# First six units' logits quad by quad, and list one-hots as 16-bit outer products with GpSimd's help

## The chip, the cores and the metric

The kernel runs on one core of a Trainium2 chip. The metric is the device time of one execution in microseconds; the median of several runs is given. TensorE (PE) multiplies matrices, VectorE (DVE) and ScalarE (ACT) work on tiles in SBUF and PSUM, GpSimd (POOL) does small copies and starts the indirect transfers, and SyncE (SP) starts most plain transfers. Each engine works its own queue in order; semaphores tie the queues together.

## The reference

```python
# x: (8, 2880, 192), 23040 tokens of 192; weight: 8 heads x 7 taps
w = softmax(weight)                                  # per head
out[b, s, h, :] = sum_k w[h, k] * x_pad[b, s + k, h, :]     # causal convolution per head
# mixture of experts: 4 groups x 4 experts, F = 1024
g_idx = argmax(x @ w_group);  g_w = softmax(x @ w_group)[g_idx]
e_idx = argmax(x @ w_expert[g_idx]);  e_w = softmax(...)[e_idx]
ye = relu(x @ w1[g, e]) @ w2[g, e]
out[token] = g_w * e_w * ye
```

Each token is convolved, sent to one of 16 experts by two argmaxes, and the expert's output is scaled by both probabilities.

## The kernel before

Tokens are taken in blocks of 120 (`BT`), and blocks in units: six units of 4, 8, 12, 8, 8 and 8 blocks, then twelve of 12 (u0 to u17). `unit(u)` is a generator whose steps are interleaved with those of other units and, later, with the experts' work; the order of instructions on each engine is fixed when the program is built.

A unit goes through these stages. Its eight heads are convolved on PE as products with a banded matrix (L452), and ACT copies them to the tile `xc` (L461). There are three `xc` buffers; u0 and u1 share one, so u4 takes the buffer of u0 and u1, u5 that of u2, u6 that of u3, and so on. Four blocks at a time (a quad), the tokens are transposed to `ta` and `tb` (`turn_a` L475, `turn_b` L483). `logits` (L495, L497) multiplies all quads of the unit by the router's weights with the weights stationary, and ACT copies the result to `lts` (L500), `logits_back` transposes it back quad by quad (L507), and ACT copies it to `lg` (L508): 20 logits for each token. DVE finds the maxima and one-hots (L539 to L551), ACT takes the Exp (L545), DVE the sums and the reciprocal (L562 to L568), which goes into `xc` as each token's factor. ACT's queue then starts the store of `xc` to `xcd` in DRAM (L570).

The lists of tokens for each expert are made as follows. A scan counts within the unit (L557), two small matmuls (L579, L580) count over the partitions, and DVE works out each token's place in the list of its expert (L583 to L595). The place is split into a row (128 of them) and a column (32). DVE makes one-hots of the row (`ohl`, L608) and of the column (`ohr`, L615), multiplies the latter by the token's number (`ohv`, L619), in halves of six blocks, and PE sums their products over the blocks (L633). The result (`lv`, `lsi`, L640, L642) is scattered by POOL to the table `idtab` (L645), at rows given by `rowi`. `rowi` (L624 to L626) needs only the counts up to the unit before, so it is placed early, and each scatter waits for the landing of the one before. The table is cleared ahead of the first scatter (`clear_table`, L269, L272, from a tile filled with a large number).

When five units are routed (`NEED`), the first portion of the lists is loaded (`idp`, L1157, SP) and POOL gathers the tokens of the first slots from `xcd` (`xg`, L717). A slot is 256 tokens of one expert: two transposes into `xa` and `xb` (L750, L752), hidden layer (L817 or L786, `ph`), relu and splitting into `hh` and `hl` (ACT, DVE, four buffers), output layer (L835, L839, or L801, L805), the factor (`ys`, L898) and POOL's scatter to `out` (L888). All matmuls of the experts are made of parts, so weights are split on arrival (`ah`, `al`, `bh`, `bl`, `cw`). From then on slots and the steps of the remaining units alternate, and after the last unit come the tail's slots.

Of the kernel before, what the change touches and what calls it, by code (L numbers as in the profile page):

```python
# [36 lines left out]
def conv_moe_kernel(  # L37
# [227 lines left out]
    fill = pa.tile([P, HB2, P], F16, name="ohl", bufs=2).rearrange("p b q -> p (b q)").bitcast(I32)  # L265
# [110 lines left out]
    quads = [-1] * QRING  # L376
    read = {-1}
# [20 lines left out]
    def gaps(u):  # L398

        return tuple(UG[3 * u:3 * u + 3]) if 3 * u < len(UG) else (GA, GL, REST)  # L400

    def unit(u, pre=None):
# [86 lines left out]
        def logits():  # L489
# [8 lines left out]
            read.add(u)  # L498
# [74 lines left out]
        while any(need <= u and pi not in idps for need, pi in needs.items()):  # L573
# [20 lines left out]
            out=posb[0:Q, 0], in0=pn, scalar1=-(LH - 1) / 2, scalar2=RND, op0=ALU.add, op1=ALU.add)  # L594
        nc.vector.scalar_tensor_tensor(  # L595
            out=posb[0:Q, 1], in0=posb[0:Q, 0], scalar=RND, in1=pn, op0=ALU.subtract, op1=ALU.subtract)

        halves = []
        for b0 in range(0, nb, HB2):
            n = min(HB2, nb - b0)  # L600
            if u >= LP and b0:
                for _ in range(HGAP):
                    yield
            ohl = pa.tile([P, HB2, P], F16, name="ohl", bufs=2)
            ohr = rt.tile([P, HB2, LH], F16, name="ohr", bufs=1)
            ohv5 = pa.tile([P, HB2, LH], F16, name="ohv", bufs=2)
            bs = slice(b0, b0 + n)
# [4 lines left out]
            if u >= LP:  # L612
                for _ in range(LG):
                    yield
            hold(u >= LP, nc.vector.tensor_tensor(  # L615
                out=ohr[0:Q, 0:n], in0=ior[0:Q].unsqueeze(1).broadcast_to([Q, n, LH]), in1=bc(posb[0:Q, 1, bs], LH),
                op=ALU.is_equal,
            ))
# [12 lines left out]
        for b0, n, ohl, ohv5 in halves:  # L631
            for k in range(n):
                nc.tensor.matmul(  # L633
                    out=pl[:, 0:nrep * LH].rearrange("p (r n) -> p r n", r=nrep), lhsT=ohl[0:Q, k],
                    rhs=ohv5[0:Q, k].unsqueeze(1).broadcast_to([Q, nrep, LH]),
                    start=b0 + k == 0, stop=b0 + k == nb - 1,
                )
# [246 lines left out]
    def finish(oo, ids, xs, hold=False, rare=False):  # L884
        ys = ff.tile([P, 2, D], F32, name="ysr" if rare else "ys", bufs=1 if rare else YB)
# [603 lines left out]
```

## Time and profile before

| what | value |
|---|---|
| median of 3 runs | 1145.09 us (1145.08 to 1145.1) |
| profiled execution | 1152.26 us, of which the profile's span is 1150.4 us |
| PE busy | 1072.8 us (93%) |
| DVE, ACT, POOL busy | 752.4, 644.1, 523.5 us |
| mean granted PE clock | 0.977 of full speed |
| transferred | 166.08 MB, mean 144 GB/s |

PE is busy for most of the span, and less so near its start. Busy shares are means over stretches with different limits, so the rows below go by stretch.

### The profile page before, as it was taken

The numbers are of one execution on the slowest core, as the hardware profiler recorded it, in microseconds if no ns is written. First come the engines' busy times: TensorE is split into PE (matmuls) and PEld (weight loads), VectorE is DVE, ScalarE is ACT, GpSimd is POOL, SyncE is SP. The second block draws the span as 40 slices with busy tenths as digits, with TensorE's granted clock in tenths as the row PEclk, the third lists the DMA queues.
The fourth block names the chain that finished last, engine by engine and source line by source line (L and its number), as shares of the span: only waits on it lengthen the run. The fifth ranks groups of instructions, "written<-read, shape, count | busy, mean of one in ns | idle before, by whom it ended". The sixth has DMA issues, their size and how long they took to land.

```text
span 1150.4 us, 20931 instructions
## 1 busy us (share of the span) xinstructions
PE 1072.8 (93%) x7124; PEld 971.1 (84%) x7124; DVE 752.4 (65%) x1671; ACT 644.1 (56%) x1362; POOL 523.5 (46%) x611
## 2 busy tenths in 40 slices
PE   6565999998999998999999999999999999999996
PEld 4444788987989998889899999999999988989986
DVE  3465878987778756576565555655556665687874
ACT  5445657765657554454455445554545555677873
POOL 3004143333334454554545454545445554487773
PEclk9878989999999999999999999999999999999998
DMA  8767688999566432332253223322333435499970
GB/s 185 186 158 228 160 222 215 252 234 216 156 155 164 122 106 85 116 112 67 83 137 113 72 76 99 113 74 73 103 101 106 133 92 157 116 257 257 252 201 19
DMA packets 143167, 166.08 MB, mean 144 GB/s; under 512 B 18946, under 2 KB 124397, under 8 KB 143054
## 3 DMA queue, kind: packets, MB, share of 16 engines
q1 hardware_dynamic: 100974, 111.04, 36.4%
q0 software_dynamic: 18752, 35.85, 10.5%
q10 hardware_dynamic: 23328, 17.80, 6.6%
q8 instruction: 57, 0.93, 0.3%
q14 instruction: 56, 0.46, 0.1%
HBM read 129.43 MB, written 36.58 MB: 144 GB/s over the span
## 4 chain that ended last, share of the span: by engine, by line
PE 70%; DMA 5%; DVE 5%; issue 4%; ACT 3%; POOL 1%; POOLq 0%; ACTq 0%; DVEq 0%
PE ph L786 21%; PE ph L817 11%; PE pm L801 7%; PE po L801 7%; PE po L835 7%; PE pm L805 3%; PE po L805 3%; PE po L839 3%; PE pm L452 3%; DMA rawc<-in_moe_w 2%; DMA xg<-xcd,idpt 2%; DVE hl L823 1%; DVE cw L698 1%; PE ph L852 1%; PE ph L750 1%
## 5 line engine op out<-in xcount | busy, mean ns | idle before, releaser
L888 POOL DMA_INDIRECT out<-ys,idp x160 | 174.3, 1090 | 267.9 <-DVE ys L898 192.0
L791 DVE SCALAR_TENSOR_TENSOR hl<-ph,hh 128x512 fp32r<-128x512 f32 x208 | 142.2, 689 | 141.7 <-ACT hh L790 141.3
L790 ACT ACTIVATE hh<-ph 128x512 fp32r<-128x512 f32 x208 | 123.0, 600 | 170.6 <-PE ph L786 167.6
L717 POOL DMA_INDIRECT xg<-xcd,idp x160 | 175.3, 1096 | 93.8 <-issue 40.5
L835 PE MATMUL po<-cw,hh 128*128 128x384 f32 x592 | 193.2, 379 | 3.0 <-DVE ys L898 3.0
L817 PE MATMUL ph<-xa,ah 128*128 128x256 f32 x592 | 169.2, 307 | 0.0
L839 PE MATMUL po<-cw,hl 128*128 128x192 f32 x592 | 149.6, 253 | 0.0
L801 PE MATMUL po<-cw,hh 128*128 128x384 f32 x416 | 134.1, 359 | 0.0
L801 PE MATMUL pm<-cw,hh 128*128 128x384 f32 x416 | 133.9, 359 | 0.0
L823 DVE SCALAR_TENSOR_TENSOR hl<-ph,hh 128x512 fp32r<-128x512 f32 x148 | 101.1, 684 | 42.7 <-ACT hh L822 42.5
L822 ACT ACTIVATE hh<-ph 128x512 fp32r<-128x512 f32 x148 | 87.9, 596 | 62.3 <-PE ph L817 49.8
L835 PEld LDWEIGHTS po<-cw,hh 128*128 128x128 f32 x592 | 112.7, 190 | 7.6 <-DVE ys L898 3.6
L817 PEld LDWEIGHTS ph<-xa,ah 128*128 128x128 f32 x592 | 113.1, 191 | 4.4 <-issue 1.5
L839 PEld LDWEIGHTS po<-cw,hl 128*128 128x128 f32 x592 | 114.4, 193 | 2.0
L805 PE MATMUL pm<-cw,hl 128*128 128x192 f32 x416 | 104.2, 250 | 0.0
L805 PE MATMUL po<-cw,hl 128*128 128x192 f32 x416 | 104.1, 250 | 0.0
L786 PE MATMUL ph<-xa,ah 128*128 128x512 f32 x208 | 86.0, 413 | 1.4 <-DVE hl L791 1.4
L698 DVE TENSOR_TENSOR cw<-rawc,cw 128x768 fp32r<-128x768 f32 x82 | 76.0, 955 | 15.1 <-ACT cw L697 14.5
L817 PE MATMUL ph<-xb,bh 128*128 128x256 f32 x296 | 84.0, 284 | 0.7 <-DVE xb L767 0.7
L805 PEld LDWEIGHTS po<-cw,hl 128*128 128x128 f32 x416 | 79.1, 190 | 5.8
L817 PE MATMUL ph<-xb,bl 128*128 128x256 f32 x296 | 83.9, 284 | 0.0
L817 PE MATMUL ph<-xa,al 128*128 128x256 f32 x296 | 83.7, 283 | 0.0
(275 smaller groups left out, 2656.2 us busy)
## 6 DMA issues: line engine op xcount, KB each, us to landing
rawc<-in_moe_w SPq DMA_DIRECT2D x82, 384.0 KB
raw<-in_moe_w SPq DMA_DIRECT2D x41, 512.0 KB
raw<-in_moe_w SPq DMA_DIRECT2D x82, 256.0 KB
xcd<-xc ACTq DMA_DIRECT2D x13, 1085.6 KB
xin<-in_x SPq DMA_DIRECT2D x7, 1134.0 KB
xc<-in_moe_w SPq DMA_DIRECT2D x18, 384.0 KB
xin<-in_x SPq DMA_DIRECT2D x6, 1039.5 KB
xin<-in_moe_w SPq DMA_DIRECT2D x9, 512.0 KB
```

What stands on the lines that cost most here:

```text
L717: nc.gpsimd.indirect_dma_start(out=xs[t][:, 0:XW], out_offset=None, in_=xcd[0:known, :], in_offset=bass.IndirectOffsetOnAxis(ap=ids[:, t, ...
L786: nc.tensor.matmul(out=hp.rearrange("p a b -> p (a b)"), lhsT=W[wgt][:, fs], rhs=xx, start=i == 0, stop=i == len(ops) - 1)
L790: nc.scalar.activation(out=hh, in_=hp, func=AF.Relu)
L791: nc.vector.scalar_tensor_tensor(out=hl, in0=hp, scalar=0.0, in1=hh.bitcast(F32), op0=ALU.max, op1=ALU.subtract,)
L801: nc.tensor.matmul(out=oo[t][:, 0:2 * D], lhsT=hh[:, ts], rhs=cw[:, f].rearrange("p a d -> p (a d)"), start=f == 0, stop=False,)
L805: nc.tensor.matmul(out=oo[t][:, 0:D], lhsT=hl[:, ts], rhs=cw[:, f, 0, :], start=False, stop=f == NF - 1,)
L817: nc.tensor.matmul(out=hp[:, j], lhsT=wgt[:, fs], rhs=xx, start=i == 0, stop=i == len(ops) - 1)
L822: nc.scalar.activation(out=hh, in_=hp, func=AF.Relu)
L823: nc.vector.scalar_tensor_tensor(out=hl, in0=hp, scalar=0.0, in1=hh.bitcast(F32), op0=ALU.max, op1=ALU.subtract,)
L835: nc.tensor.matmul(out=oo[t][:, 0:2 * D], lhsT=hh[:, j, ts], rhs=cw[:, f].rearrange("p a d -> p (a d)"), start=f == 0, stop=False,)
L839: nc.tensor.matmul(out=oo[t][:, 0:D], lhsT=hl[:, j, ts], rhs=cw[:, f, 0, :], start=False, stop=f == NF - 1,)
L888: nc.gpsimd.indirect_dma_start(out=outviews[nscat[0] % len(outviews) if view is None else view], out_offset=bass.IndirectOffsetOnAxis(ap=i ...
```

## The change

Three things are changed. For the first six units (`UROW`), `logits_of` takes each quad by itself: four matmuls with the block's tokens stationary (the router's 20 columns are repeated five times) and two for the tail of the features put the logits with tokens on partitions, so that `lts` and the transposes back are not needed, and ACT copies each quad straight to `lg`. The wait for a free place in `ta` and `tb` is then taken quad by quad.

The row's one-hot is made as a product: the one-hot of the expert (`ohp`, a copy of `ohx` by POOL with blocks in pairs innermost) times the one-hot of the row within the expert's eight (`oh8`), which carries the token's number too. It is one 16-bit instruction for the whole unit. `ohr` is one 16-bit instruction as well, and `ohv` is gone. `rows` is one instruction with an accumulated sum, and `rowi` becomes a cast on POOL. The tile that clears the table takes an `hl` buffer; the rare path's `ysr` does too (not shown).

```diff
-    fill = pa.tile([P, HB2, P], F16, name="ohl", bufs=2).rearrange("p b q -> p (b q)").bitcast(I32)
+    fill = ff.tile([P, 2, SLOT], F32R, name="hl", bufs=HB).rearrange("p a b -> p (a b)").bitcast(I32)
...
+    REPL = 5
+    UROW = 6
...
-        while any(v not in read for v in quads[k:k + NQ]):
+        prior = quads[k:k + NQ]
+        while u >= UROW and any(v not in read for v in prior):
             yield
...
+        def logits_of(q):
+            lgp = bank("l")
+            for i in range(HQ):
+                o = lgp[0:BT, 2 * i * REPL * NL:2 * (i + 1) * REPL * NL].rearrange("p (j n) -> p j n", j=2)
+                for j in range(2):
+                    nc.tensor.matmul(
+                        out=o[:, j].rearrange("p (r n) -> p r n", n=NL), lhsT=ta[:, q, 2 * i + j],
+                        rhs=wr[:, 0, 0:NL].unsqueeze(1).broadcast_to([P, REPL, NL]), start=j == 0, stop=False)
+                nc.tensor.matmul(
+                    out=o[:, :, 0:NL], lhsT=tb[:, q, i], rhs=wrb[:, :, 0:NL], start=False, stop=True)
+            read.add((u, q))
+            nc.scalar.activation(
+                out=lg[0:BT, q * QB:(q + 1) * QB],
+                in_=lgp[0:BT, 0:QB * REPL * NL].rearrange("p (b n) -> p b n", b=QB)[:, :, 0:NL], func=AF.Copy)
...
-            for k, f in ((ga, turn_a), (ga + 1, turn_b)):
+            for k, f in ((ga, turn_a), (ga + 1, turn_b), (ga + gl, logits_of))[0:3 if u < UROW else 2]:
                 events.setdefault(k + 3 * q, []).append((f, q))
-        for k, f in ((0, logits), (2, logits_back)):
+        for k, f in ((0, logits), (2, logits_back)) if u >= UROW else ():
...
+        ohp = rt.tile([P, E * UB], F16, name="ohp")[:, 0:E * nb].rearrange("p (a e i) -> p a e i", e=E, i=BI)
+        nc.gpsimd.tensor_copy(out=ohp[0:Q].rearrange("p a e i -> p e a i"), in_=ohf[0:Q].rearrange("p e (a i) -> p e a i", i=BI))
...
-            hold(u >= LP, nc.vector.tensor_tensor(
-                out=ohl[0:Q, 0:n], in0=iop[0:Q].unsqueeze(1).broadcast_to([Q, n, P]), in1=bc(posb[0:Q, 0, bs], P),
-                op=ALU.is_equal,
-            ))
...
-            hold(u >= LP, OHE.tensor_tensor(
-                out=ohv5[0:Q, 0:n], in0=ohr[0:Q, 0:n], in1=bc(vals[0:Q, bs], LH), op=ALU.mult))
+        row8 = rt.tile([P, UB], I32, name="row8", bufs=1)[:, 0:nb]
+        nc.vector.tensor_scalar(
+            out=row8[0:Q], in0=posb[0:Q, 0].bitcast(I32), scalar1=VS // LH - 1, scalar2=None, op0=ALU.bitwise_and)
...
+        nc.vector.tensor_tensor(out=oh8[0:Q], in0=over(row8[0:Q], LE), in1=iol[0:Q].unsqueeze(1).broadcast_to([Q, NP, LE, BI]), op=ALU.is_equal)
+        nc.vector.tensor_tensor(out=oh8[0:Q], in0=oh8[0:Q], in1=over(vals[0:Q, 0:nb], LE), op=ALU.mult)
...
+        hold(u >= LP, nc.vector.tensor_tensor(
+            out=ohl[0:Q], in0=ohp[0:Q].unsqueeze(3).broadcast_to([Q, NP, E, LE, BI]),
+            in1=oh8[0:Q].unsqueeze(2).broadcast_to([Q, NP, E, LE, BI]), op=ALU.mult,
+        ))
...
+        hold(u >= LP, nc.vector.tensor_tensor(
+            out=ohr[0:Q], in0=ior[0:Q].unsqueeze(1).broadcast_to([Q, NP, LH, BI]), in1=over(posr[0:Q], LH), op=ALU.is_equal))
...
-        nc.vector.tensor_tensor(out=rows[:, 0:E], in0=eo, in1=sel, op=ALU.mult)
-        nc.vector.tensor_reduce(out=rows[:, E:E + 1], in_=rows[:, 0:E], axis=AX.X, op=ALU.add)
-        nc.vector.tensor_tensor(out=rowi, in0=rows[:, E:E + 1], in1=goff, op=ALU.add)
+        nc.vector.scalar_tensor_tensor(
+            out=rows[:, 0:E], in0=eo, scalar=goff, in1=sel, op0=ALU.add, op1=ALU.mult, accum_out=rows[:, E:E + 1])
+        nc.gpsimd.tensor_copy(out=rowi, in_=rows[:, E:E + 1])
```

Three places show how the queues are laid. The first is DVE, about the lists of u1, before. `mx_599` is the first instruction of u2's softmax; DMASW6 is the landing of the first scatter.

```order
L608 TENSOR_TENSOR ohl_537<-iop_153,posb_534 120x768
L615 TENSOR_TENSOR ohr_538<-ior_156,posb_534 120x192 [waits DVE_49]
L608 TENSOR_TENSOR ohl_543<-iop_153,posb_534 120x256 [waits DMAHW5_49,DMAHW4_49]
L619 TENSOR_TENSOR ohv_539<-ohr_538,vals_147 120x192 [waits DVE_49]
L626 TENSOR_TENSOR rowi_690<-rows_689,goff_165 128x1 [waits DMASW6_49]
L224 MEMSET xin_727 6x192 [waits DMAHW2_49]
L615 TENSOR_TENSOR ohr_544<-ior_156,posb_534 120x64 [waits DVE_49]
L619 TENSOR_TENSOR ohv_545<-ohr_544,vals_147 120x64 [waits DVE_49]
L640 TENSOR_SCALAR lv5_563<-pm_554 128x32 [waits PE_49]
L642 SCALAR_TENSOR_TENSOR lsi_564<-pm_554,lv5_563 128x32 [waits DVE_49]
L539 TENSOR_REDUCE mx_599<-lg_426 120x60 [waits Activation_49]
L540 TENSOR_TENSOR dd_600<-lg_426,mx_599 120x240 [waits DVE_49]
```

In the changed kernel, the same place on DVE. `ohl_588` is u1's, `oh_623`, `ohx_634` and `ss_624` are u2's; Pool is the counter of GpSimd's finished work.

```order
L567 TENSOR_TENSOR oh_623<-sc_622,mx_620 120x240
L629 TENSOR_TENSOR oh8_585<-row8_583,iol_152 120x64 [waits DVE_49]
L640 TENSOR_TENSOR ohr_589<-ior_158,posh_581 120x256
L630 TENSOR_TENSOR oh8_585<-oh8_585,vals_147 120x64 [waits DVE_49]
L571 TENSOR_TENSOR ohx_634<-oh_623 120x192
L633 TENSOR_TENSOR ohl_588<-ohp_480,oh8_585 120x1024 [waits DVE_49,Pool_49]
L579 SCALAR_TENSOR_TENSOR cum_638<-keep12_135,ohx_634 120x192 [waits DVE_49]
L584 TENSOR_REDUCE ss_624<-dd_621 120x60 [waits Activation_49]
```

Before, `rowi_690` with its wait for the scatter stood ahead of u1's last one-hots and of u2's softmax; now u2's softmax is spread around u1's `ohl`, which waits for POOL, and no instruction here waits for a scatter.

The second is POOL, from the first scatter on, before:

```order
L645 DMA idtab_88<-lsi_415,rowi_405 377088x1 [waits DMAHW4_49,DMAHW5_49,DVE_49,Pool_49]
L645 DMA idtab_88<-lsi_564,rowi_550 377088x1 [waits DMASW6_49,DVE_49]
L645 DMA idtab_88<-lsi_708,rowi_690 377088x1 [waits DMASW7_49,DMASW0_49,DVE_49]
L645 DMA idtab_88<-lsi_870,rowi_856 377088x1 [waits DMASW1_49,DMASW0_49,DVE_49]
L645 DMA idtab_88<-lsi_972,rowi_958 377088x1 [waits DMASW1_49,DVE_49]
L717 DMA xg0_211<-xcd_87,idp0_976 128x193 [waits DMAHW6_49,DMAHW7_49,DMAHW4_49,DMAHW1_49]
```

And now (`rowi_593` and `ohp_480` are made in u0's and u1's steps, `rowi_728` is the row index of u2, `ohp_636` the experts' one-hots of u2):

```order
L646 CAST rowi_593<-rows_592 128x1 [waits DVE_49]
L577 CAST ohp_480<-ohx_478 120x16x4x2 [waits DVE_49]
L665 DMA idtab_88<-lsi_413,rowi_404 377088x1 [waits DMAHW5_49,DMAHW4_49]
L646 CAST rowi_728<-rows_727 128x1 [waits DMASW6_49,DVE_49]
L577 CAST ohp_636<-ohx_634 120x16x6x2 [waits DVE_49,Pool_49]
L665 DMA idtab_88<-lsi_606,rowi_593 377088x1 [waits DVE_49,Pool_49]
L577 CAST ohp_684<-ohx_682 120x16x4x2 [waits DVE_49,Pool_49]
L646 CAST rowi_805<-rows_804 128x1 [waits DMASW7_49,DVE_49]
L665 DMA idtab_88<-lsi_745,rowi_728 377088x1 [waits DMASW0_49,DVE_49,Pool_49]
L646 CAST rowi_965<-rows_964 128x1 [waits DMASW0_49,DVE_49]
L665 DMA idtab_88<-lsi_818,rowi_805 377088x1 [waits DMASW1_49,DVE_49,Pool_49]
L577 CAST ohp_878<-ohx_876 120x16x4x2 [waits DVE_49]
```

POOL had only scatters and gathers here; now `rowi` and `ohp` stand among them, and `rowi_728` waits for the first scatter's landing ahead of `ohp_636`.

The third is ACT, behind the store of u1 (`xc_224`), before. `xc_581` is u4's tile, which waits for the stores of u0 and u1; `lg_426` is u2's.

```order
L570 DMA xcd_87<-xc_224 120x8x193 [waits DMAHW7_49,DVE_49]
L500 ACTIVATE lts_579<-ph_570 128x360 [waits PE_49]
L484 ACTIVATE tb_208<-po_617 128x240 [waits PE_49]
L484 ACTIVATE tb_208<-ph_643 128x240 [waits PE_49,Activation_49]
L461 ACTIVATE xc_581<-ph_582 120x8x24 [waits DMAHW7_49,DMAHW6_49]
L461 ACTIVATE xc_581<-po_621 120x8x24
L476 ACTIVATE ta_207<-pm_585 128x480 [waits PE_49]
L461 ACTIVATE xc_581<-pm_591 120x8x24 [waits PE_49]
L508 ACTIVATE lg_426<-pm_594 120x240 [waits PE_49]
L461 ACTIVATE xc_581<-ph_640 120x8x24
```

And now, from the last quad of u2's logits (`lg_432`) on; `xc_640` is u4's tile, `dd_621` u2's Exp, `xc_341` u2's store and `lg_528` u3's logits.

```order
L525 ACTIVATE lg_432<-po_557 120x80 [waits PE_49]
L487 ACTIVATE tb_207<-ph_565 128x240 [waits PE_49]
L525 ACTIVATE lg_528<-po_610 120x80 [waits PE_49]
L463 ACTIVATE xc_640<-ph_641 120x8x24 [waits DMAHW7_49,DMAHW6_49,PE_49]
L463 ACTIVATE xc_640<-po_662 120x8x24 [waits PE_49]
L565 ACTIVATE dd_621<-dd_621 120x240 [waits DVE_49]
L463 ACTIVATE xc_640<-ph_688 120x8x24 [waits PE_49]
L463 ACTIVATE xc_640<-po_698 120x8x24 [waits PE_49]
L463 ACTIVATE xc_640<-pm_651 120x8x24 [waits PE_49]
L592 DMA xcd_87<-xc_341 120x12x193 [waits DMAHW4_49,DVE_49]
L525 ACTIVATE lg_528<-pm_654 120x80 [waits PE_49]
```

Before, u4's copies stood ahead of u2's logits; now u2's logits and half of u3's stand ahead of them, and u2's Exp and store shortly behind.

## Rows read from the trace of the kernel before

**Rows 1.** busy time of each engine, x instructions, PE clock, DMA share and rate, by stretch.

```profile
0.00:125.00 125.00, 80.88 (x521) 60.49 (x522) 70.08 (x279) 61.98 (x169) 24.36 (x46) 0.86 0.74 187
150.00:925.00 775.00, 761.62 (x5033) 697.71 (x5033) 507.09 (x1104) 420.63 (x895) 353.27 (x454) 0.99 0.47 128
```

**Rows 2.** waits, 0 to 120: engine, line, what for; total us, times, longest.

```profile
ACT xc L461 <- DMA xcd<-xc: 19.8, 4, 8.8
...
DVE rowi L626 <- DMA idtab<-lsi,rowi: 8.2, 1, 8.2
```

**Rows 3.** timeline of ScalarE: start us, us, instruction [idle before <- releaser]; ACTq issues DMAs.

```profile
25.17 0.37 ACT L484 ACTIVATE tb<-ph 128x240 f32<-128x240 f32 x1
...
31.12 0.32 ACT L508 ACTIVATE lg<-pm 120x160 f32<-120x160 f32 x1
...
34.88 0.33 ACTq L570 DMA_DIRECT2D xcd<-xc  x1
...
42.05 0.33 ACT L461 ACTIVATE xc<-ph 120x192 f32<-120x192 f32 x1 [4.13 <-DMA raw<-in_moe_w]
...
52.58 0.39 ACT L545 ACTIVATE dd<-dd 120x240 f32<-120x240 f32 x1
...
55.22 0.32 ACTq L570 DMA_DIRECT2D xcd<-xc  x1
...
62.42 0.56 ACT L461 ACTIVATE xc<-ph 120x192 f32<-120x192 f32 x2 [1.40 <-DMA xcd<-xc]
...
65.36 0.32 ACTq L570 DMA_DIRECT2D xcd<-xc  x1
...
74.43 0.42 ACT L461 ACTIVATE xc<-ph 120x288 f32<-120x288 f32 x1 [7.07 <-DMA xcd<-xc]
...
79.25 0.32 ACTq L570 DMA_DIRECT2D xcd<-xc  x1
...
87.11 0.42 ACT L461 ACTIVATE xc<-ph 120x288 f32<-120x288 f32 x1 [2.55 <-DMA xcd<-xc]
...
96.60 0.32 ACTq L570 DMA_DIRECT2D xcd<-xc  x1
...
109.99 0.42 ACT L461 ACTIVATE xc<-ph 120x288 f32<-120x288 f32 x1 [8.79 <-DMA xcd<-xc]
```

**Rows 4.** timeline of TensorE.

```profile
30.39 0.38 PE L507 MATMUL pm<-ident,lts 128*120 128x128 f32 x2
```

**Rows 5.** timeline of GpSimd.

```profile
38.38 1.05 POOL L645 DMA_INDIRECT idtab<-lsi,rowi  x1 [24.19 <-DVE ohv L619]
...
90.39 1.84 POOL L645 DMA_INDIRECT idtab<-lsi,rowi  x1 [18.71 <-DVE xin L224]
97.93 1.83 POOL L717 DMA_INDIRECT xg<-xcd,idp  x1 [5.70 <-DMA idp<-idtab]
```

**Rows 6.** timeline of SyncE.

```profile
94.61 0.39 SPq L1157 DMA_DIRECT2D idp<-idtab  x1
```

**Rows 7.** timeline of VectorE.

```profile
46.49 0.16 DVE L626 TENSOR_TENSOR rowi<-rows,goff 128x1 int32<-128x1 f32 x1 [8.22 <-DMA idtab<-lsi,rowi]
...
56.73 0.95 DVE L608 TENSOR_TENSOR ohl<-iop,posb 120x768 f16<-120x768 f32 x1
```

**Rows 8.** timeline of TensorE, the first hidden matmul.

```profile
117.87 0.50 PE L817 MATMUL ph<-xa,ah 128*128 128x256 f32 x1
```

**Rows 9.** groups by line, GpSimd: busy us, mean ns | idle before.

```profile
L733 POOL COPY xg<-xg 128x64 f32<-128x64 f32 x64 | 17.5, 274 | 70.1 <-DMA xg<-xcd,idp 70.1
```

**Rows 10.** the stretch with the loop of stores, columns as in Rows 1.

```profile
33.00:117.00 84.00, 50.37 (x319) 34.98 (x317) 49.16 (x183) 36.91 (x96) 15.70 (x14) 0.80 0.68 183
```

**Rows 11.** the chain that ended last: start us, us, what.

```profile
130.63 7.95 DMA idtab<-lsi,rowi
238.87 11.69 DMA rawc<-in_moe_w
265.81 15.98 DMA rawc<-in_moe_w
```

More of the change, by code (lines that the diff above doesn't have):

```diff
@@ L24 @@
 QB = 4
+BI = 2
 SLOT = 256
@@ L373, in conv_moe_kernel @@
     QRING = 4
+    REPL = 5
+    UROW = 6
     tall = const.tile([P, QRING, QB, BT], F32, name="ta")
     tbll = const.tile([P, QRING, QB // 2, BT], F32, name="tb")
-    quads = [-1] * QRING
-    read = {-1}
+    quads = [(-1, 0)] * QRING
+    read = {(-1, 0)}
     wrb = const.tile([P, 2, NC], F32, name="wrb")
@@ L466, in unit @@
         k = min(range(QRING - NQ, -1, -1), key=lambda k: max(quads[k:k + NQ]))
-        while any(v not in read for v in quads[k:k + NQ]):
+        prior = quads[k:k + NQ]
+        while u >= UROW and any(v not in read for v in prior):
             yield
-        quads[k:k + NQ] = [u] * NQ
+        quads[k:k + NQ] = [(u, q) for q in range(NQ)]
         ta, tb = tall[:, k:k + NQ], tbll[:, k:k + NQ]
@@ L497, in logits @@
                         nc.tensor.matmul(out=o, lhsT=wrb[:, g % 2], rhs=tb[:, :, g // 2], start=False, stop=True)
-            read.add(u)
+            read.update((u, q) for q in range(NQ))
             lgt = pa.tile([P, 512], F32, name="lts", bufs=2)
@@ L520, in unit @@
             for f, *q in events.get(k, []):
+                while f is turn_a and prior[q[0]] not in read:
+                    yield
                 f(*q)
@@ L594, in unit @@
             out=posb[0:Q, 0], in0=pn, scalar1=-(LH - 1) / 2, scalar2=RND, op0=ALU.add, op1=ALU.add)
+        posr = rt.tile([P, UB], F16, name="posh")[:, 0:nb]
         nc.vector.scalar_tensor_tensor(
[L596 to L607, printed above, removed]
-            hold(u >= LP, nc.vector.tensor_tensor(
-                out=ohl[0:Q, 0:n], in0=iop[0:Q].unsqueeze(1).broadcast_to([Q, n, P]), in1=bc(posb[0:Q, 0, bs], P),
-                op=ALU.is_equal,
-            ))
[L612 to L618, printed above, removed]
-            hold(u >= LP, OHE.tensor_tensor(
-                out=ohv5[0:Q, 0:n], in0=ohr[0:Q, 0:n], in1=bc(vals[0:Q, bs], LH), op=ALU.mult))
-            halves.append((b0, n, ohl, ohv5))
@@ new lines, in unit, with over @@
+            out=posr[0:Q], in0=posb[0:Q, 0], scalar=RND, in1=pn, op0=ALU.subtract, op1=ALU.subtract)
+        row8 = rt.tile([P, UB], I32, name="row8", bufs=1)[:, 0:nb]
+        nc.vector.tensor_scalar(
+            out=row8[0:Q], in0=posb[0:Q, 0].bitcast(I32), scalar1=VS // LH - 1, scalar2=None, op0=ALU.bitwise_and)
+        NP = nb // BI
+        oh8 = rt.tile([P, UB // BI, LE, BI], F16, name="oh8", bufs=1)[:, 0:NP]
+        def over(a, n):
+            return a.rearrange("p (a i) -> p a i", i=BI).unsqueeze(2).broadcast_to([Q, NP, n, BI])
@@ L622, in unit @@
+        if u >= LP:
+            for _ in range(HGAP):
+                yield
+        hold(u >= LP, nc.vector.tensor_tensor(
+            out=ohr[0:Q], in0=ior[0:Q].unsqueeze(1).broadcast_to([Q, NP, LH, BI]), in1=over(posr[0:Q], LH), op=ALU.is_equal))
         rows = rt.tile([P, E + 1], F32, name="rows")
         rowi = rt.tile([P, 1], I32, name="rowi")
-        nc.vector.tensor_tensor(out=rows[:, 0:E], in0=eo, in1=sel, op=ALU.mult)
-        nc.vector.tensor_reduce(out=rows[:, E:E + 1], in_=rows[:, 0:E], axis=AX.X, op=ALU.add)
@@ L630, in unit @@
         nrep = REPO if u < REPU else 1
[L631 to L637, printed above, removed]
+        for k in range(nb):
+            nc.tensor.matmul(
+                out=pl[:, 0:nrep * LH].rearrange("p (r n) -> p r n", r=nrep),
+                lhsT=ohl[0:Q, k // BI, :, :, k % BI].rearrange("p e l -> p (e l)"),
+                rhs=ohr[0:Q, k // BI, :, k % BI].unsqueeze(1).broadcast_to([Q, nrep, LH]),
+                start=k == 0, stop=k == nb - 1,
+            )
         lv5 = rt.tile([P, LH], F32, name="lv5", bufs=1)
```

24 lines of the change are left out of this document (14 added, 10 removed).

## Prediction

> **What bounds the kernel now.** I read the stretches first, then the waits of the opening, then the queues of the engines that wait there. In [rows 1] TensorE (PE) is busy 761.62 of the 775 us from 150 to 925: there, work saved on another engine buys nothing. In the first 125 us it is busy only 80.88, so 44 us are idle there, and this is where an edit can pay. [rows 2] say what the opening waits for: ScalarE's (ACT) copies into `xc` stood 19.8 us, in four waits, for stores `xcd<-xc` to land, and VectorE (DVE) stood 8.2 us in one wait at `rowi`, for a list scatter.
>
> [rows 3] show the first as a loop. With three `xc` buffers, unit u+3 may copy its convolution only when unit u's store has landed; ACT is in order, so what stands behind that copy, the next units' logits and Exp, waits too, and the Exp gates the next store. Store of u1 (34.88), first copy of u4 (42.05, flight 7.17); store of u2 (55.22), copy of u5 (62.42, flight 7.20); u3 65.36 to 74.43 (9.07); u4 79.25 to 87.11 (7.86); u5 96.60 to 109.99 (13.39). The flights sum to 44.7 us. Behind the last one come the first slot's transposes and, at 117.87 [rows 8], its first hidden matmul, 7.9 us later. A second chain runs beside it: list scatters, each behind the landing of the one before (38.38 to 46.49, 8.1 us [rows 5, 7]), the last at 90.39, the list's load at 94.61 [rows 6], the first gather at 97.93 [rows 5].
>
> The link that is no flight stands out in the loop: from u4's copy at 42.05 to u2's store at 55.22 are 13.2 us. DVE's `rowi` for u2 waits until 46.49 for scatter 0 [rows 7], and u1's remaining one-hots and all of u2's softmax are queued behind it; only then comes Exp at 52.58 and the store 2.64 us later [rows 3].
>
> **The change, part by part.**
> (1) *Logits by quad.* For u1, the last `tb` copy stands at 25.17, the transposes back at 30.39 [rows 4], the logits' copy `lg` at 31.12 [rows 3]: 5.95 us, most of it between engines. One quad's six matmuls and one copy instead let `lg` end near 28; the gain lies between 0.4 (the transposes alone) and about 3.5. I take 3.0, since the queues of PE and ACT place the quad's pieces directly behind its transposes. Store of u1: 34.88 - 3.0 = 31.9; landing, flight 7.2, 39.1.
> (2) *`rowi` to GpSimd (POOL).* In the new order u2's whole softmax stands on DVE ahead of anything that waits for a scatter, so at 39.1 u2's Exp needs only ACT. Store of u2: 39.1 + 0.4 (one copy) + 2.6 = 42.1, against 55.22. This is 13 us, 3 from (1) and 10 from (2).
> (3) *The loop from there.* u2's store has 12 blocks, u1's 8, and the engines are full then, so I take 7.17 x 12/8 = 10.8 rather than the old 7.2: landing 52.9. u3's Exp now stands ahead of that copy, its store behind it: 53.3, flight 9.07, landing 62.4 (was 74.43). Behind it come u4's last quad, softmax, Exp and store; u1 took 3.76 from `lg` to store, so +4.2 is 66.6; flight 9.07 rather than 7.86, since idle engines helped the old one: 75.7. u5: u4's row from landing to store, 4.82 with weight copies between, gives 80.5; flight 13.39: 93.9, against 109.99, 16.1 us earlier.
> (4) *The list chain.* Four scatters at about 8.7 each behind 38.38 put the last at 73.1, the load at 77.3 (4.2 later, as before) and the first gather at 80.6, against 97.93. It runs ahead of the store loop, so the loop decides.
> (5) *What collides.* In 33 to 117 the DMA engines are busy 0.68 of 84 us [rows 10]: 27 us are idle. A stretch shortened by 16 leaves 11. I charge 3 us beyond the lengthened flights of (3), between 0 and the 22 worked out under the first rival. So 13.1 us are left at the first hidden matmul: 104.8 for 117.87.
> The Trainium skill ("DMA: Bandwidth & Descriptors", section "Issuing engines are not separate DMA queues") says that transfers started by ScalarE, SyncE and GpSimd run on the same 16 engines and interleave, which speaks against the change: an earlier store takes its time from the weight loads. The trace agrees: two stores of 8 blocks took 7.17 and 13.39 us [rows 3].
> (6) *One-hots.* For 12 blocks two `ohl` instructions of 0.95 [rows 7] become one that costs between 0.95 (twice the rate) and 1.9 (the same rate). Either way it is not above the old pair, and small `oh8`, `row8` replace `ohv` and two of the row instructions. DVE does not bind after 150, where PE hides it; counted 0. GpSimd's new `ohp` has three times the elements of its 274 ns copy [rows 9], so 0.27 to 0.82; POOL has the room. Behind a waiting `rowi` on POOL stand the next `ohp`, and so DVE's `ohl`, and the next scatter, which had to wait for that landing anyway; the store loop does not pass through them. If POOL is late, the second rival below applies.
> (7) *Behind the opening.* PE follows with the same work and 98% busy [rows 1], so the 13.1 are carried to the end. One old stall of the chain is a scatter's landing that DVE's `rowi` waits for, 7.95 long from 130.63 [rows 11]; it passes to POOL, which may give 2 to 5 more. Against it stand two waits of that chain for weight loads, 11.69 and 15.98 long [rows 11], which shift earlier only if the loads do: each load waits for a buffer that a slot frees, so they should. I set these two against each other.
>
> Sum: -16.1 + 3 = -13.1. On the profiled execution, 1152.26 - 13.1 = 1139.2; the median of the runs, 1145.09, lies 7.2 below that execution, and the same 13.1 gives **1132.0**.
>
> **Rivals.**
> *The transfers take it back.* For: the engines are full in bursts, and u5's flight is already 13.39. If all five flights take that, they sum to 67 instead of my 49.9, 17 more: the loop is where it was, and 1145. If half of that comes, or the weight loads near 240 to 280 stay where they were in part, the time is about 1140. Against: 27 idle us. Chance 0.18, most of it near 1140.
> *GpSimd becomes late, and the kernel slower.* `ohp` now stands on POOL among the gathers and the scatters of `out`, which wait for DVE's `ys`; before, DVE needed nothing from POOL for the lists. If DVE reaches `ohl` before POOL reaches `ohp`, DVE's `hl` stand behind it and PE runs dry. Twelve units (u6 to u17) meet slots. At 3 us for each, 36 us outweigh the 13: 1168. It decides from 1.3 us a unit, (13.1 + 2.3) / 12. Against: in the new order `ohp` is many DVE instructions ahead of its `ohl`, in the units that I looked at. Chance 0.10, mostly just past that point, 1148 to 1160.
> *The stall only moves.* If DVE's `ohl` of u1, which waits for POOL, is reached while POOL still waits for the landing, u2's counts and store stay behind it, and only the 3 us of the logits are left: 1142. Against: u1's `ohp` stands ahead of that wait on POOL. Chance 0.08.
> *More than forecast.* Flights as short as before (44.7 instead of 49.9), no other collision (3), and the 7.95 wait gone (up to 5): 13 more, 1119; half of it 1126. Chance 0.10.
>
> **How the numbers follow.** My forecast, 1127 to 1138, holds 0.54; with the cases above, faster by over 0.2% (2.3 us, about what a measurement of this kernel can tell from none; below 1142.8) has 0.85: 0.54, 0.10, 0.16 of the first rival and 0.05 of the third. Within it lie 0.05 (0.02 and 0.03). Slower has 0.10. For 8 in 10 the range leaves out the best twentieth, below 1122, and the slower rival: **1122 to 1144**.
>
> **What would show it.** In the changed profile: no wait of DVE for `idtab`; POOL's `rowi` takes it. u1's `lg` near 28; the stores of u2 to u5 near 42, 53, 67 and 80, their flights 7 to 13. The list's load near 77, the first hidden matmul near 105, and from there the old distance to the end. Wrong would be: DVE waiting for POOL's `ohp` in the slots by over 1 us a unit; flights all near 13; or PE idle near 240 to 280 grown by what the opening gained.

## The result and the profile after

The changed kernel's median is 1125.7 us (1125.15 to 1127.44, 4 runs), against 1145.09 us (1143.7 to 1145.1, 4 runs) before: ratio 0.9843, 95% interval 0.9829 to 0.9858, 19.4 us less. The forecast was 1132.0, 13.1 us less, in a range of 1122 to 1144; the gain is half as large again as forecast. The profiled execution has a span of 1123.9 us, against 1150.4 us; a second profile of the kernel before (first experiment below) has 1143.5 us, so that some 7 of the 26.5 us between the first two spans belong to that one execution. "Second profile" below means this one.

The stretches of the changed kernel, with the columns of [rows 1]:

```profile
0.00:125.00 125.00, 97.35 (x699) 84.10 (x700) 78.33 (x304) 72.71 (x191) 33.88 (x66) 0.95 0.84 213
150.00:900.00 750.00, 741.18 (x4887) 679.26 (x4886) 479.18 (x1047) 404.49 (x863) 354.91 (x465) 1.00 0.47 126
```

PE does 97.35 us of work in the first 125 us, where it did 80.88 [rows 1]; from 150 on it is busy about 99%, as it was 98% before. The DMA engines are busier at the start, 0.84.

ScalarE's queue in the changed kernel, which answers to [rows 3] (start us, us, instruction):

```profile
29.59 0.24 ACT L525 ACTIVATE lg<-pm 120x80 f32<-120x80 f32 x1 [0.30 <-PE pm L522]
...
33.19 0.33 ACTq L592 DMA_DIRECT2D xcd<-xc  x1
...
42.60 0.34 ACT L463 ACTIVATE xc<-ph 120x192 f32<-120x192 f32 x1 [3.10 <-DMA xcd<-xc]
...
44.86 0.32 ACTq L592 DMA_DIRECT2D xcd<-xc  x1
...
52.85 0.34 ACT L463 ACTIVATE xc<-pm 120x192 f32<-120x192 f32 x1 [5.11 <-DMA xcd<-xc]
52.93 0.32 ACTq L592 DMA_DIRECT2D xcd<-xc  x1
...
64.66 0.32 ACTq L592 DMA_DIRECT2D xcd<-xc  x1
...
76.72 0.32 ACTq L592 DMA_DIRECT2D xcd<-xc  x1
```

The stores of u1 to u5 start at 33.19, 44.86, 52.93, 64.66 and 76.72; the forecast had 31.9, 42.1, 53.3, 66.6 and 80.5. u1's store takes until 42.60, 9.4 us, not the 7.2 that were assumed; u2's lands after 8.0, not 10.8. Only two copies still wait for a store.

GpSimd and SyncE, which answer to [rows 5, 6]:

```profile
41.98 0.84 POOL L646 CAST rowi<-rows 128x1 int32<-128x1 f32 x1 [7.17 <-DMA idtab<-lsi,rowi]
...
71.11 1.14 POOL L665 DMA_INDIRECT idtab<-lsi,rowi  x1 [4.51 <-DVE xin L225]
...
84.01 1.08 POOL L737 DMA_INDIRECT xg<-xcd,idp  x1 [8.69 <-DMA idp<-idtab]
```

```profile
76.97 0.39 SPq L1180 DMA_DIRECT2D idp<-idtab  x1
77.41 5.13 SPq L228 DMA_DIRECT2D xin<-in_x  x2
```

The wait for the first scatter is now POOL's (7.17 us at `rowi`), and VectorE (DVE) has none. The last of the five scatters starts at 71.11 (90.39 before), the lists' load at 76.97 (94.61), the first gather at 84.01 (97.93). From scatter to gather are 12.9 us, where before there were 7.5: 1.6 of the difference is the scatter's landing and 3.7 the load. It starts 0.25 us behind u5's store (76.72) here and 2.0 us ahead of it before (96.60 [rows 3]); between load and gather the DMA engines are busy 0.81, before 0.51.

TensorE at the end of the opening (the brackets give the idle time ahead and what ended it):

```profile
88.96 1.29 PE L454 MATMUL ph<-xin,band 126*120 126x288 f32 x2 [8.34 <-DMA xin<-in_x]
94.01 0.33 PE L770 MATMUL pm<-ident,xg 128*128 128x128 f32 x1 [0.25 <-DMA xg<-xcd,idp]
...
101.05 0.36 PE L837 MATMUL ph<-xa,ah 128*128 128x256 f32 x1
```

The first hidden matmul is at 101.05, against 117.87 [rows 8] and 113.36 in the second profile. A new wait stands here: 8.34 us for u8's input, whose load SyncE issues behind the lists' load (77.41 above). The gathered tokens come right behind it: TensorE waits 0.25 us more for them at 94.01. Before, the last waits ahead of the first hidden matmul were these, in the first profile and in the second:

```profile
110.71 1.44 PE L633 MATMUL pm<-ohv,ohl 120*128 120x192 f16 x8 [8.62 <-ACT lg L508]
```

```profile
101.90 1.44 PE L633 MATMUL pm<-ohv,ohl 120*128 120x192 f16 x8 [3.35 <-ACT lg L508]
105.07 0.45 PE L750 MATMUL pm<-ident,xg 128*128 128x128 f32 x1 [1.74 <-DMA xg<-xcd,idp]
...
113.36 0.49 PE L817 MATMUL ph<-xa,ah 128*128 128x256 f32 x1
```

The copy `lg` of the first row stands on ScalarE behind the copy that waited for u5's store [rows 3, 109.99]. So in the first profile that landing held the first slot; in the second it came at 101.18 and the gathered tokens came last.

### The profile page after: what moved, and what is told of

It is laid out like the page before. It is cut to its first block, busy times and chain, and to the rows that moved or that the text cites. A ratio compares the mean times of both kernels' runs of the same rounds, so it can differ in the third digit from the quotient of the medians.

```text
span 1123.9 us, 21046 instructions
## 1 busy us (share of the span) xinstructions
PE 1071.0 (95%) x7160; PEld 977.9 (87%) x7160; DVE 730.9 (65%) x1637; ACT 640.9 (57%) x1362; POOL 538.3 (48%) x647
## 4 chain that ended last, share of the span: by engine, by line
PE 75%; DMA 10%; DVE 6%; issue 4%; ACT 3%; POOL 1%; SPq 0%; POOLq 0%; ACTq 0%; DVEq 0%
PE ph L806 21%; PE ph L837 11%; PE pm L821 7%; PE po L855 7%; PE po L821 7%; PE pm L454 3%; PE pm L825 3%; PE po L825 3%; PE po L859 3%; DMA xg<-xcd,idpt 2%; DMA rawc<-in_moe_w 2%; DMA xcd<-xc 2%; DMA xg<-xcd,idp 1%; PE pm L478 1%; PE ph L872 1%
```

## The experiments

The theory to be tested (A) was the prediction's: VectorE's wait at `rowi` held u2 up and carried 10 of the 13 us, u1's quads 3. Rival B gave the gain to the quads, rival C to the one-hots' shorter VectorE time. After the first four kernels A was changed to A2: the quads pay wherever a store or an Exp waits for logits, rowi on VectorE costs again among the first slots, the one-hots nothing. Theory D was added from the trace: the lists' load sets the opening's end, and TensorE's wait for u8's input is on the path to the first slot.

All times are compared with runs of the kernel before on the same chip. This table sums up what the traces show; the last column is the span less the start of the first hidden matmul.

| kernel | ratio (95% interval) | u0's store | u2's store | u5's store | last of 5 scatters | first gather | first hidden | behind it |
|---|---|---|---|---|---|---|---|---|
| before, second profile | 1.0011 (0.9980 to 1.0043) | 23.67 | 53.48 | 93.32 | 87.94 | 95.35 | 113.36 | 1030.1 |
| rowi on GpSimd alone | 0.9966 (0.9930 to 1.0003) | 21.31 | 48.78 | 87.01 | 80.92 | 93.53 | 110.61 | 1029.9 |
| quads alone | 0.9969 (0.9936 to 1.0002) | 23.43 | 45.79 | 82.64 | 76.06 | 89.38 | 107.87 | 1037.0 |
| lists alone | 0.9959 (0.9927 to 0.9990) | 21.79 | 46.61 | 84.30 | 78.24 | 90.86 | 108.21 | 1030.7 |
| changed, rowi back on DVE | 0.9929 (0.9905 to 0.9954) | 19.88 | 42.73 | 79.76 | 73.44 | 87.91 | 106.75 | 1028.5 |
| quads and rowi, old one-hots | 0.9916 (0.9889 to 0.9944) | 20.13 | 43.88 | 78.90 | 72.96 | 86.32 | 103.97 | 1026.4 |
| lists, quads for u0 and u1 | 0.9879 (0.9850 to 0.9908) | 20.26 | 44.81 | 79.11 | 70.47 | 81.91 | 100.09 | 1022.3 |
| changed | 0.9843 (0.9829 to 0.9858) | 22.27 | 44.86 | 76.72 | 71.11 | 84.01 | 101.05 | 1022.9 |
| changed, second profile | 0.9835 (0.9801 to 0.9869) | 20.26 | 45.10 | 78.03 | 72.43 | 85.40 | 103.14 | 1024.2 |
| changed, ohp on DVE | 0.9813 (0.9789 to 0.9838) | 23.77 | 47.37 | 79.83 | 73.94 | 82.83 | 102.12 | 1022.6 |
| changed, list load by GpSimd | 0.9954 (0.9936 to 0.9972) | 22.96 | 46.19 | 78.18 | 72.68 | 90.61 | 108.39 | 1029.7 |
| changed, u8's input by GpSimd | 0.9907 (0.9878 to 0.9936) | 20.59 | 43.13 | 76.69 | 72.09 | 87.79 | 106.14 | 1024.9 |
| changed, quads for all units | 0.9973 (0.9946 to 1.0000) | 20.95 | 45.11 | 77.06 | 72.15 | 83.81 | 100.16 | 1039.6 |

The times are of one execution each. The changed kernel's two profiles differ by 2.0 us at u0's store already, and two profiles of one kernel by 2.1 and 4.5 us at the first hidden matmul; smaller differences between two rows show little by themselves.

The first hidden matmul comes 16.4 to 19.3 us behind the first gather in every row (19.9 in the first profile), while the gathers themselves move by 13.4. Behind u5's store it comes 20.0 to 30.2 us. With the quads alone, u5's store comes 10.7 us earlier than in the second profile of before, the first gather 6.0 and the first hidden matmul 5.5. In twelve of the fourteen profiles the gathered tokens are the last thing that TensorE waits for ahead of the first slot. The exceptions are the first profile of before (the landing of u5's store, above) and the changed kernel with ohp on DVE (u8's input, below). So in these kernels the list chain mostly sets the first slot, and in the kernel before it ran level with the stores.

**The kernel before once more.** Edit: none.

> The kernel before once more, unchanged, for a second profile, since its first profiled execution was 7.2 us longer than the median of its runs. If the 26.5 us between the two spans are all the change's, this profile's span is again near 1150; if part was that one execution's, the span is near 1143 and the places where it is shorter show which. Time: the same as before, within 0.2%.

Measured: 1148.18 us, ratio 1.0011, span 1143.5. The first profile's opening was 4.5 us longer (117.87 against 113.36), the rest 2.4. Differences of traces are taken from this second profile from here on.

**Only rowi moved.** Edit, in the kernel before:

```diff
-        nc.vector.tensor_tensor(out=rows[:, 0:E], in0=eo, in1=sel, op=ALU.mult)
-        nc.vector.tensor_reduce(out=rows[:, E:E + 1], in_=rows[:, 0:E], axis=AX.X, op=ALU.add)
-        nc.vector.tensor_tensor(out=rowi, in0=rows[:, E:E + 1], in1=goff, op=ALU.add)
+        nc.vector.scalar_tensor_tensor(
+            out=rows[:, 0:E], in0=eo, scalar=goff, in1=sel, op0=ALU.add, op1=ALU.mult, accum_out=rows[:, E:E + 1])
+        nc.gpsimd.tensor_copy(out=rowi, in_=rows[:, E:E + 1])
```

> The kernel before with only the row index moved: rows in one instruction, rowi cast by GpSimd. Theory A (VectorE's wait at rowi held up u2's softmax and store, 10 of the 13 us that I worked out at the opening): 1133 to 1138, u2's store near 45 instead of 55. Rival B (the logits by quad carry the gain): 1142 or more. Rival C (the 16-bit one-hots' saved VectorE time carries it): 1142 or more.

Measured: 1142.98 us, ratio 0.9966, with 1 in the interval; u2's store at 48.78. Theory A expected 1133 to 1138. Of the 4.7 us at u2's store, 2.4 stand at u0's store already, which `rowi` does not hold up. VectorE's queue shows why so little came:

```profile
44.30 0.17 DVE L567 SCALAR_TENSOR_TENSOR se<-se,sg 120x12 f32<-120x12 f32 x1
48.43 0.17 DVE L583 TENSOR_TENSOR off<-po,eoff 128x16 f32<-128x16 f32 x1 [3.96 <-PE po L580]
48.52 0.22 DVE L568 RECIPROCAL xc<-se 120x12 f32<-120x12 f32 x1
```

u2's sums are done at 44.30, but the reciprocal that its store needs stands behind `off`, which waits 3.96 us for the matmul that counts. One wait of DVE gave way to the next.

**Only the quads.** Edit: of the change's diff, `logits_of`, `UROW`, `prior` and the events; all of the lists as before.

> The kernel before with only the logits quad by quad. Theory A: rowi's wait still stands on VectorE, so only the 3 us of u1's logits, 1140 to 1144. Rival B: 1126 to 1132. Rival C: 1143 to 1146.

Measured: 1144.96 us, ratio 0.9969. In time this is near theory A's 1140 to 1144, but not for its reason: u2's store is 7.7 us earlier, not 3, and the first hidden matmul 5.5. It is lost again behind it, 1037.0 against 1030.1. The chain of waits (start us, us, what) and the two stretches:

```profile
121.65 7.59 DMA idtab<-lsi,rowi
...
141.44 9.42 DMA idtab<-lsi,rowi
```

```profile
125.00:150.00 25.00, 21.07 (x141) 17.90 (x140) 18.05 (x54) 12.49 (x27) 7.13 (x5) 0.93 0.61 166
150.00:175.00 25.00, 21.47 (x161) 19.05 (x160) 17.94 (x41) 15.18 (x31) 10.66 (x9) 0.93 0.54 150
```

Two scatters' landings that DVE's `rowi` waits for now lie on the path among the first slots (one in [rows 11]), and PE stands idle 7.5 of 50 us (3.6 in the second profile of before).

**Only the lists.** Edit, in the changed kernel:

```diff
-    UROW = 6
+    UROW = 0
```

> The changed kernel with the logits as before for all units (UROW = 0). Theory A: as with rowi alone, 1130 to 1137, and within 3 us of it. Rival B: 1141 or more. Rival C: 1126 to 1132, and well below rowi alone.

Measured: 1143.97 us, ratio 0.9959: not A's 1130 to 1137, and no better than rowi alone within the intervals. Neither half carries the gain. Added up, the halves give 0.7%; together they gave 1.6%.

**rowi back on VectorE.** Edit, in the changed kernel:

```diff
-        nc.gpsimd.tensor_copy(out=rowi, in_=rows[:, E:E + 1])
+        nc.vector.tensor_copy(out=rowi, in_=rows[:, E:E + 1])
```

> The changed kernel with only rowi's cast given back to VectorE, where it waits for a scatter's landing. Theory A2 (VectorE's wait at rowi costs a few us at the opening and again 5 to 10 among the first slots, where it took back what the quads alone had gained): 1134 to 1142, with VectorE waits for idtab of 5 us or more in sum and PE idle of 6 us or more between 125 and 175. Rival C (the 16-bit one-hots' shorter VectorE time is what pays beside the quads): 1125 to 1130.

Measured: 1137.08 us, ratio 0.9929, as theory A2 said. The chain of waits has the two landings back:

```profile
119.35 7.50 DMA idtab<-lsi,rowi
...
138.29 9.01 DMA idtab<-lsi,rowi
```

Between 125 and 175 PE is idle 5.8 us (6 or more were expected; 1.3 in the changed kernel). Of the 11.3 us that its span is longer than the changed kernel's, 5.7 lie ahead of the first hidden matmul and 5.6 behind it (3.6 and 4.3 against the changed kernel's second profile). u2's store is not later: 42.73, against 44.86 and 45.10 with `rowi` on GpSimd.

**ohp on VectorE.** Edit, in the changed kernel: `nc.gpsimd.tensor_copy(out=ohp...` becomes `nc.vector.tensor_copy(out=ohp...`.

> The changed kernel with the experts' one-hots ohp made by VectorE instead of GpSimd. If GpSimd's part in the lists neither helps nor hurts (theory A2): within 3 us of the changed kernel, 1123 to 1129. If VectorE waits for a late GpSimd: 1116 to 1122. If VectorE's time among the slots binds: 1129 or more.

Measured: 1123.52 us, ratio 0.9813. Its interval overlaps those of the changed kernel, so no difference is shown: that GpSimd's part in the one-hots helps or hurts is not seen. The cast takes DVE 0.25 us (POOL took 0.57 for the same 192 elements):

```profile
L577 DVE CAST ohp<-ohx 120x192 f16<-120x192 bf16 x13 | 3.2, 248 | 0.0
```

In this profile the lists' load starts 0.57 us ahead of u5's store, and the first gather follows after 3.6 us. Then TensorE's last wait is for u8's input, and none for the gathers follows:

```profile
79.26 0.39 SPq L1180 DMA_DIRECT2D idp<-idtab  x1
79.83 0.32 ACTq L592 DMA_DIRECT2D xcd<-xc  x1
82.83 1.06 POOL L737 DMA_INDIRECT xg<-xcd,idp  x1 [7.75 <-DMA idp<-idtab]
90.35 1.28 PE L454 MATMUL ph<-xin,band 126*120 126x288 f32 x2 [6.92 <-DMA xin<-in_x]
```

**The lists' load by GpSimd.** Edit, in the changed kernel:

```diff
-    IQ = nc.sync
+    IQ = nc.gpsimd
```

> The changed kernel with the lists' load idp issued by GpSimd, behind the last scatter, instead of by SyncE, where u8's input and the weights are queued behind its wait. If TensorE's 8.3 us wait for u8's input at 80.6 is on the path (new theory D: the list's load, not the stores, now sets the opening's end, and what is queued behind it arrives late): that wait falls to 3 us or less, the first hidden matmul comes at 95 to 98 instead of 101, and the time is 1119 to 1123. If the gathers set the first slot anyway: first hidden at 100 to 102, 1124 to 1127.

Measured: 1139.79 us, ratio 0.9954, 14 us slower than the changed kernel and outside both expectations. PE's wait for u8's input fell from 8.34 to 0.85 us, as expected, but another took its place:

```profile
82.94 0.72 PE L454 MATMUL ph<-xin,band 126*120 126x288 f32 x2 [0.85 <-DMA xin<-in_x]
...
97.82 0.45 PE L770 MATMUL pm<-ident,xg 128*128 128x128 f32 x1 [12.35 <-DMA xg<-xcd,idp]
```

```profile
79.34 1.03 POOL L1180 DMA_DIRECT2D idp<-idtab  x1 [5.53 <-DMA idtab<-lsi,rowi]
...
90.61 1.08 POOL L737 DMA_INDIRECT xg<-xcd,idp  x1 [9.92 <-DMA idp<-idtab]
```

With SyncE no longer held by the lists' load, inputs and weights start ahead of it, and from the start of this load of 10 KB to the first gather are 11.3 us, where there were 7.0; the profile's busy share of the DMA engines over that time is 1.08, where it was 0.81. So SyncE's wait had kept other loads from running into it. How much of the 4.3 us lies in the load's going through GpSimd's queue was not tried apart.

**Quads for all units.** Edit, in the changed kernel: `UROW = 18`.

> The changed kernel with all 18 units' logits quad by quad. Theory A2 (the quads pay where the next store or Exp waits for the logits, at the opening; behind it TensorE has other work): 1124 to 1130. If shorter logits pay everywhere: 1115 to 1122. If the extra matmul time of twelve units on the busy TensorE counts: 1127 to 1135.

Measured: 1141.53 us, ratio 0.9973, 16 us slower than the changed kernel and outside all three expectations. The opening is as short as the changed kernel's (100.16), but PE's busy time on the page is

```profile
PE 1093.4 (96%) x7364; PEld 1014.5 (89%) x7364; DVE 731.1 (64%) x1637; ACT 642.6 (56%) x1374; POOL 538.6 (47%) x647
```

22.4 us more than the 1071.0 of the changed kernel, 1.9 for each of the twelve units. Where PE is the bound, the quads are dearer than the two-step logits; in the first six units PE had idle time for them.

**u8's input by GpSimd.** Edit, in the changed kernel:

```diff
-        hold(nc.sync.dma_start(out=xin[0:R, off + k0:off + nb, :], in_=src))
+        hold((nc.gpsimd if v == 8 else nc.sync).dma_start(out=xin[0:R, off + k0:off + nb, :], in_=src))
```

> The changed kernel with u8's input load issued by GpSimd ahead of the last of the five scatters, not by SyncE behind the lists' load. Theory D: TensorE's 8.3 us wait for it is on the path, and the lists' load, which keeps its free engines here, lands as before; first hidden matmul 95 to 98 for 101.05, time 1119 to 1123. If the gathers set the first slot: first hidden 99 to 102, 1124 to 1128. If the earlier megabyte delays the lists' load as in the run before: first hidden 104 or more, 1132 or more.

Measured: 1132.91 us, ratio 0.9907. The third case came true: the megabyte is started just ahead of the last scatter, whose landing then takes 12.2 us (to `rowi` at 84.34) instead of 5.9 (71.11 to 76.97 in the changed kernel), and the lists' load starts at 84.33.

```profile
70.50 1.29 POOL L228 DMA_DIRECT2D xin<-in_x  x1 [3.98 <-DVE lsi L662]
72.09 1.03 POOL L665 DMA_INDIRECT idtab<-lsi,rowi  x1 [0.31 <-issue]
...
84.34 0.18 POOL L646 CAST rowi<-rows 128x1 int32<-128x1 f32 x1 [9.05 <-DMA idtab<-lsi,rowi]
```

Whether the scatter was held by sharing GpSimd's queue or by sharing the engines was not tried. PE's wait for u8's input fell to 0.85 us in the kernel above and to at most 2.9 here; both kernels are slower, since the gathers come later (by 6.6 and 3.8 us), and the first hidden matmul with them (7.3 and 5.1). That bears out theory D's first half (the list chain sets the end of the opening). Its second half (that wait is on the path) is not settled: in the changed kernel PE works from the end of that wait until 0.25 us before the gathered tokens land, so that taking away the wait alone gains nothing; with ohp on DVE, where the gathers came earlier, it was the last wait.

**Quads for u0 and u1 only.** Edit, in the changed kernel: `UROW = 2`.

> The changed kernel with the logits quad by quad for u0 and u1 only (UROW = 2). My prediction's step (1), 3 us from u1's logits alone: 1124 to 1129. If each unit's logits stand between a landing and the next store (theory A2): 1134 to 1142, close to the lists alone.

Measured: 1129.04 us, ratio 0.9879: the quads of the first two units give 0.8% beside the lists, those of the other four 0.4% more, which lies within the intervals. That is the upper edge of what was expected from step (1), 1124 to 1129; A2's 1134 to 1142 was wrong.

**Quads and rowi, old one-hots.** Edit: the diff of the second experiment on top of the quads alone.

> The kernel before with the logits quad by quad and rowi on GpSimd, but the old one-hots. Theory A2 (these two edits are the change's gain): 1124 to 1130. Rival C (the one-hots' saved time is needed too): 1132 to 1140.

Measured: 1134.03 us, ratio 0.9916, so the 16-bit one-hots (with the buffer for clearing the table) give another 0.7% beside the two: A2's 1124 to 1130 was wrong, and rival C, which alone explained nothing, has a part. TensorE waits 11.5 us for gathers ahead of its first slot here (8.3 us for u8's input in the changed kernel):

```profile
PE pm L770 <- DMA xg<-xcd,idp: 11.5, 2, 11.2
```

**The changed kernel once more.** Edit: none.

> The changed kernel once more, unchanged, beside the other three: 1123 to 1128, first hidden matmul at 100 to 103. A time well above would mean that its place depends on the chip or the run.

Measured: 1126.92 us, ratio 0.9835; the first hidden matmul at 103.14. The gain is there again. The spans of two profiles of one kernel differ by 3.4 us here and by 6.9 before.

## Why the prediction was right, and where it was not

**Place and sign were right.** The opening was where PE stood idle, and it got shorter. 104.8 was forecast for the first hidden matmul, worked from the first profile; 101.05 and 103.14 came. That is 16.8 and 14.7 us less than in that profile, 12.3 and 10.2 less than in the second, for 13.1 forecast. u5's store came at 76.72 (80.5 forecast), the lists' load at 76.97 (77.3), and what was won there stayed to the end. That the sum came so near is partly luck, as (1), (2) and (4) below were off.

**The shares of (1) and (2) were not.** I gave the logits 3 us and rowi 10 at u2's store. Measured, the quads alone move that store by 7.7, rowi alone by 4.7, both and the one-hots by 8.6. Counted from u0's store, to take out the different starts, u2's comes after 31.2 and 29.8 us before, after 27.5 with rowi alone, 22.4 with the quads alone, 22.6 and 24.8 in the changed kernel, and 22.9 with rowi back on DVE. So at this store the quads bring nearly all, and beside them rowi on GpSimd brings nothing that the profiles show. The wait at rowi was not the only thing behind which u2 stood: with it gone DVE waited for the counting matmul, and the logits behind u4's copy were late by themselves. I had read one wait at the head of a queue as the whole delay of what is queued behind it.

**(4), that the list chain runs ahead of the stores, was wrong for the changed kernel.** For the execution that I read, the first profile, the row at 109.99 did hold the first slot: behind it PE waited for no gather. In the second profile the gathers already came last. In the changed kernel no copy waits for the stores of u3 to u5 any more. Its chain that ended last (start us, us, what) has, from u0's store to the gathers, one landing of a store and then the list chain:

```profile
33.19 9.31 DMA xcd<-xc
...
71.11 5.73 DMA idtab<-lsi,rowi
...
76.97 6.24 DMA idp<-idtab
...
85.39 8.58 DMA xg<-xcd,idp
```

I forecast u5's landing for 93.9; the gathered tokens landed at 94.0. That these two agree is luck. The stores matter since u4's copies, and so its list, stand behind u1's. The chain was well sized up to its load; from the last scatter to the gather it took 12.9 us, not the 7.5 taken over from before. That is a collision as in step (5), 5.4 us, at a place where I had charged none; the 3 us charged elsewhere stood in for part of it. What the load collides with can be read from the profiles: where SyncE started it 0.5 us or more ahead of u5's store (before, ohp on DVE, quads for u0 and u1), or 7.6 us behind it (u8's input by GpSimd), the first gather came 3.3 to 3.6 us later; where it started 0.1 to 1.2 us behind that store, 5.3 to 8.1. What the prediction drew from the Trainium skill ("DMA: Bandwidth & Descriptors", section "Issuing engines are not separate DMA queues"), that transfers of different issuing engines interleave on the same 16 engines, is borne out there: ScalarE's store delays SyncE's load.

Two figures of the prediction's working are slips that change little: the five flights of (3) sum to 49.5, not 49.9, and of the 22 us named in (5) only 17 lie beyond the lengthened flights.

**(6) held.** `ohl` for 12 blocks takes 0.955 us, the lower end:

```profile
L633 DVE TENSOR_TENSOR ohl<-ohp,oh 120x1536 f16<-120x1536 f16 x13 | 12.4, 955 | 1.3 <-DVE oh L630 0.5
```

That the one-hots count for 0, though, was wrong: 0.7% lies between the kernels with and without them. Of the spans' 6.5 us, 2.9 lie ahead of the first hidden matmul and 3.5 behind it (0.8 and 2.2 of 3.1 against the changed kernel's second profile). Why they count was not tried.

**(7), nothing behind the opening, was the mis-sized term.** Behind the first hidden matmul the changed kernel needs 1022.9 us and 1024.2, the kernel before 1032.5 and 1030.1: 5.9 to 9.7 more, 7.2 with the profiles used here. This term, forecast as nothing, separates the forecast from the result. One part is seen by taking it back: with rowi on DVE, two landings are on the path again and the changed kernel needs 4.3 to 5.6 us more there; with the quads alone, two landings are on the path as well and the stretch takes back all that was won ahead of it (6.9 for 5.5). I had put them at 2 to 5 and set them against the weight loads; that the weights took as much was assumed, and no run shows it. The rest I can place only in part. From the first hidden matmul to 550 PE idles 15.5 us in the second profile of before and 10.5 in the changed kernel. These are two stretches of the second profile of before, and then of the changed kernel:

```profile
125.00:150.00 25.00, 21.65 (x158) 19.15 (x157) 19.46 (x52) 11.46 (x25) 8.73 (x6) 0.93 0.64 166
425.00:475.00 50.00, 44.68 (x306) 42.05 (x305) 30.99 (x72) 22.94 (x49) 28.58 (x40) 0.97 0.35 103
```

```profile
125.00:150.00 25.00, 23.68 (x185) 21.11 (x183) 19.10 (x49) 15.41 (x35) 11.33 (x10) 1.00 0.94 236
425.00:475.00 50.00, 47.04 (x281) 42.12 (x280) 28.25 (x66) 23.42 (x50) 33.96 (x50) 1.00 0.31 91
```

PE idles 2.0 us less in the first and 2.4 less in the second, where the last units make way for the tail; in the second stretch kernels without quads idle 5.0 us or more, those with quads 4.2 or less, and why was not tried. Why rowi on GpSimd without the quads (1029.9, 1030.7) wins nothing behind the opening, and with them 7, stays open.

**The rivals.** "The transfers take it back" happened in part (5.4 us from the last scatter to the gather) and for good in the two kernels that moved a load. "The stall only moves" is what rowi alone did. GpSimd was not late: the changed kernel's trace has no wait of DVE for `ohp`. How it would look is to be seen in the kernel where GpSimd also issues the lists' load; there, among its waits (engine, line, what for; total us, times, longest), stands

```profile
DVE ohl L633 <- POOL ohp L577: 5.7, 1, 5.7
```

once in the whole span, and PE waits 3.8 us for `hl` behind it. In the changed kernel with ohp on DVE, where this wait cannot arise, no gain is shown.

## What to carry to other kernels

A wait at the head of an in-order queue bounds what its removal gives from above, as far as that queue goes: look for the next wait of the same consumer before counting it, and for what the removed wait kept away from shared engines. Edits that each pay little can pay together, and one edit's gain can be eaten by a stall that another edit removes, so they are tried together before one is dropped. What sets the start of a stage is read from the last wait ahead of it, in more than one profile of the kernel: here two profiles of one kernel name two different waits. A candidate that keeps its distance to the start over several kernels while the others move is a second sign. And times of two profiles are best counted from a point ahead of what the edit touches, since two executions of one kernel were 2.0 us apart at the first store already.

## What the hardware showed that was not expected

A load of 10 KB was followed by its first gather after 3.3 to 3.6 us when it started ahead of a store from another queue or long behind it, and after 5.3 to 8.1 us when it started 0.1 to 1.2 us behind that store; issued by GpSimd behind inputs, weights and that store, after 11.3. A scatter's landing went from 5.9 to 12.2 us behind one load of a megabyte from the same queue.

A 16-bit product of 120x1536 with pairs innermost took 0.955 us on VectorE, as long as a comparison of half as many elements with a 32-bit operand [rows 7]; 8 blocks, 1024 elements, took 0.693, so 512 more cost 0.26 us. The 16-bit `ohv` of before, one of whose operands is broadcast innermost, took 0.35 us for 192 elements, like its 32-bit neighbour `ohr`, and 0.22 for 64, so 128 more cost 0.13 us, twice as much for each. That the broadcast makes the difference was not tried apart. The same cast of 192 elements took VectorE 0.25 us and GpSimd 0.57.
